# Segment 0's x comes in transposed by three DMA transposes, with wq beside them on ScalarE's queue, in place of four TensorE transposes and one DMA transpose

## The chip, the core and the metric

The kernel runs on one core of a Trainium2 chip. The core has five engines that run side by side, each with its own instruction queue in a fixed order: TensorE (PE, matmuls), VectorE (DVE), ScalarE (ACT, activation functions and copies), GpSimd (POOL) and SyncE (SP, which issues DMAs here). Engines wait for each other by semaphores. The metric is the device time of one execution in microseconds; 262.3 us is the median of three runs before the change, and lower is better.

## The reference

The input x has 2048 tokens of 512 features in bf16. It goes through two branches, and a gate per token mixes their results. Branch a is an attention with a memory, over 4 segments of 512 tokens, with 32 heads of 16 features; branch b is a gated feed-forward layer.

```python
q, k, v = x @ wq, x @ wk, x @ wv            # split into 32 heads and 4 segments of L = 512
for s in range(4):
    logits = einsum('bhqd,bhkd->bhqk', qs, ks) * scale + mask   # mask: only earlier keys
    a_dot = softmax(logits) @ vs
    a_mem = (phi(qs) @ M) / (phi(qs) @ z + 1e-6)
    o = g_head * a_mem + (1 - g_head) * a_dot
    M, z = M + phi(ks).T @ vs, z + phi(ks).sum()
a = concat(o) @ wo
b = (relu(x @ W_gate) * (x @ W_up)) @ W_down
g = sigmoid((x * gate_w).sum(-1))
return g * a + (1 - g) * b
```

## The kernel before

**Layout.** P is 128, D is 512, F is 1792, NC = 4 is the number of 128-row chunks of D. A matmul contracts over the 128 partitions, so the projections need x with features on the partitions: xT[seg % 3] holds one segment as 128 partitions by 4 chunks by 512 tokens. The natural layout, xn (tokens on the partitions), is needed only for the token gate: gate_tasks (L441) multiplies it by gate_w on DVE (L447), four instructions per segment.

**What is computed from xT.** proj_q, proj_k and proj_v (L567, L596, L626) make Q, K and V of a segment, with four accumulating matmuls of 512 columns for each 128 output rows, one per chunk of D. The sum lands in one of the 8 PSUM banks, and a copy on DVE or ACT brings it to SBUF and frees the bank (QT at L588, ktr at L606, Vp at L637). K is then spread into KT by three masked products on DVE (L609). attention (L718) has, for each group u of eight heads, score matmuls (L685, visits of 8 or more small matmuls, on row tiles of PE), exponentials on ACT (L714), a causal mask on POOL (L730) and the product with V on column tiles of PE (L757). ffn_tasks (L915) computes the two hidden projections of branch b from xT, multiplies them on DVE into hT (L931), and out_tile (L942) sums W_down and wo in one bank, scales it (L961) and writes a tile of the output.

**How the order is made.** The kernel does not issue instructions as the Python code runs. Each piece of work is a Task, added to a Plan with its engine and its dependencies. ORDER (L31) is a list of all task numbers, written out by hand, and UNITS (L97) a string that says which buffer or PSUM bank each task's slot takes. Plan.run emits the tasks in that order, which fixes each engine's own order. A matmul task that is marked flexible and stands between column-tiled work is emitted as four column tiles of 32 output rows (L497) and otherwise as one whole matmul (L493). LANDS (L272) holds the times at which the loads were expected when the order was made; it emits nothing.

**The loads.** DMAs at the start are issued in the order of the code, before any task. SP's queue has, in this order: half 0 of xn (tokens 0 to 255, features 0 to 255), wq chunk 0, the first half of wk, wq chunks 2 and 3, a DMA transpose of features 256 to 511 of segment 0 into xT, the second half of wk, wv, the first pieces of W_gate and W_up (g0, u0), gate_w, beta, g1, u1, the rest of xn (all tokens, features 256 to 511), the DMA transpose of segment 1, and the last pieces of W_gate and W_up. ACT's queue has tokens 256 to 511 of xn's first features and wq chunk 1.

**The start of segment 0.** PE first runs seven matmuls on constants (heat, L1002). Then x0_tasks (L522) turns features 0 to 255 on PE: eight matmuls of 128 columns against an identity (L531), each pair into one PSUM bank, a filler matmul of 256 columns on zeros (L540), and four copies, two on DVE and two on ACT (L546), that bring the banks to xT. proj_q for segment 0 runs chunk 0 for all four output groups, then chunk 1, both from the turned half; chunks 2 and 3 wait for the DMA transpose and stand behind K matmuls that use the first two chunks.

## Time and profile before

| | |
|---|---|
| median of 3 runs | 262.3 us (261.94 to 262.34) |
| the profiled execution, its own time | 262.61 us |
| span of that execution in the profile | 260.9 us |
| busy: PE, DVE, ACT, POOL | 97%, 77%, 70%, 26% of the span |
| first matmul, start of the last matmuls | 0.84 us, 257.72 us |
| moved by DMA | 19.75 MB, mean 76 GB/s |

The span goes from the first to the last event that the profiler recorded; the execution's own time has some 1.7 us around it. Busy time is the union of an engine's instructions. Records of consecutive matmuls overlap (at L493 they are mostly 0.38 us long and start 0.215 us apart), so the distance between starts, not the length, is what each one costs. The chain of the work that ended last is followed back from the end, from each instruction to what released it. A wait is put down to the last of the semaphores that it needed. In the rows of stages there stand, after the stretch and its length, the busy time and number of instructions of PE, of its weight loads, DVE, ACT and POOL, then the granted clock, the share of the 16 DMA engines and their GB/s.

### The profile page before, as it was taken

What the parts mean: (1) busy time and instruction counts of PE and PEld (TensorE: products, weight loads), DVE (VectorE), ACT (ScalarE), POOL (GpSimd) and SP (SyncE); (2) the same over time, 40 slices, a digit from 0 to 9 for tenths busy, and PEclk for the clock granted to TensorE, in tenths of its full rate; (3) what the DMA queues carried; (4) which work ended last, traced back from release to release, by engine and by line L of the source; (5) the groups of instructions that cost most, each with busy time, mean ns of one, the idle gap of its engine ahead of it and who ended that gap; (6) DMA issues with size and microseconds to landing.
All of it is one profiled execution on the core that took longest, in us unless ns stands there. A gap on an engine that the chain in (4) does not pass through costs nothing.

```text
span 260.9 us, 9058 instructions
## 1 busy us (share of the span) xinstructions
PE 254.1 (97%) x3914; PEld 120.7 (46%) x3942; DVE 202.1 (77%) x452; ACT 183.0 (70%) x186; POOL 67.3 (26%) x188
## 2 busy tenths in 40 slices
PE   8999999999999999999999999999999999999995
PEld 3444444444545444454545444444545444445445
DVE  2499889999888957998998894697888736596622
ACT  3199899998889678797377837989477875793000
POOL 8018742224322213113021242124112422112000
PEclk9999999999999999999999999999999999999999
DMA  7999963030006243300016541000000043000011
GB/s 194 314 284 259 283 140 105 3 68 13 3 23 132 64 114 75 68 3 3 15 35 107 167 110 57 4 0 8 14 0 10 7 145 112 0 3 3 3 40 43
DMA packets 31600, 19.75 MB, mean 76 GB/s; under 512 B 16072, under 2 KB 30024, under 8 KB 31560
## 3 DMA queue, kind: packets, MB, share of 16 engines
q1 hardware_dynamic: 31144, 18.90, 28.6%
q8 instruction: 31, 0.51, 0.9%
q10 hardware_dynamic: 416, 0.26, 0.3%
q14 instruction: 9, 0.07, 0.1%
HBM read 13.21 MB, written 2.55 MB: 60 GB/s over the span
## 4 chain that ended last, share of the span: by engine, by line
PE 97%; issue 1%; DVE 0%
PE ps L493 53%; PE ps L497 25%; PE ps L685 9%; PE ps L757 7%; PE ps L1006 1%; PE ps L880 1%; PE ps L855 0%; PE ps L531 0%; PE ps L814 0%; DVE osr L961 0%; PE ps L540 0%
## 5 line engine op out<-in xcount | busy, mean ns | idle before, releaser
L714 ACT ACTIVATE E<-ps 128x2048 bf16<-128x2048 f32 (+3 forms) x79 | 120.4, 1552 | 26.4 <-PE ps L685 25.6
L730 POOL TENSOR_SCALAR_AFFINE_SELECT E<-E 128x256 bf16<-128x256 bf16 x128 | 53.7, 448 | 155.0 <-ACT E L714 149.1
L931 DVE TENSOR_TENSOR hT<-ps,rgr 128x512 bf16<-128x512 f32 x56 | 37.8, 681 | 21.9 <-PE ps L493 13.5
L925 ACT ACTIVATE rgr<-ps 128x512 bf16<-128x512 f32 x56 | 32.7, 596 | 20.3 <-PE ps L493 11.1
L493 PE MATMUL ps<-xT,wu_sb 128*128 128x512 bf16 x158 | 41.9, 380 | 0.6 <-issue 0.5
L493 PE MATMUL ps<-xT,wg_sb 128*128 128x512 bf16 x132 | 34.9, 379 | 0.6 <-issue 0.3
L493 PE MATMUL ps<-wd_sb,hT 128*128 128x512 bf16 (+2 forms) x147 | 29.5, 339 | 1.4 <-issue 1.3
L685 PE MATMUL ps<-QT,KT 32*128 32x64 bf16 (+3 forms) x768 | 27.8, 244 | 0.0
L788 DVE STREAM_TRANSPOSE T<-ps 128x512 f32<-128x512 f32 x32 | 21.9, 701 | 3.5 <-PE ps L757 3.1
L497 PE MATMUL ps<-wd_sb,hT 128*32 128x512 bf16 x384 | 24.0, 380 | 0.0
L493 PEld LDWEIGHTS <-wu_sb 128*128 128x128 bf16 x164 | 14.9, 98 | 18.5 <-issue 2.5
L497 PE MATMUL ps<-xT,wg_sb 128*32 128x512 bf16 x344 | 23.1, 380 | 0.0
L685 PEld LDWEIGHTS <-KT 32*128 32x128 bf16 x768 | 11.0, 92 | 24.1 <-issue 22.8
L961 DVE TENSOR_SCALAR osr<-ps,ngcol 128x512 bf16<-128x512 f32 (+2 forms) x18 | 12.2, 682 | 11.3 <-PE ps L493 10.4
L493 PEld LDWEIGHTS <-wg_sb 128*128 128x128 bf16 x138 | 12.9, 98 | 15.7 <-issue 1.3
L493 PEld LDWEIGHTS <-hT 128*128 128x128 bf16 x156 | 13.5, 98 | 14.1 <-issue 2.3
L757 PE MATMUL ps<-E,Vp 128*17 128x320 bf16 (+3 forms) x512 | 19.1, 273 | 0.0
L714 ACT ACTIVATE Em<-ps 128x2048 bf16<-128x2048 f32 (+2 forms) x11 | 15.6, 1415 | 4.3 <-PE ps L685 4.1
L497 PE MATMUL ps<-xT,wu_sb 128*32 128x512 bf16 x240 | 16.2, 379 | 0.0
L588 DVE CAST QT<-ps 128x512 bf16<-128x512 f32 x16 | 10.9, 684 | 6.0 <-PE ps L493 5.5
L493 PE MATMUL ps<-xT,wq_sb 128*128 128x512 bf16 x49 | 14.3, 407 | 0.2 <-issue 0.2
L493 PE MATMUL ps<-wv_sb,xT 128*128 128x512 bf16 x54 | 13.9, 379 | 0.4 <-issue 0.3
(100 smaller groups left out, 308.7 us busy)
## 6 DMA issues: line engine op xcount, KB each, us to landing
out_dram<-osr SPq DMA_DIRECT2D x15, 128.0 KB
xn<-in_A_x_dram SPq DMA_DIRECT2D x3, 512.0 KB
xn<-coefs SPq DMA_DIRECT2D x6, 256.0 KB
cdr<-coefs SPq DMA_DIRECT2D x6, 256.0 KB
wg_sb<-in_B_W_gate_dram SPq DMA_DIRECT2D x2, 512.0 KB
wu_sb<-in_B_W_up_dram SPq DMA_DIRECT2D x2, 512.0 KB
wd_sb<-in_B_W_down_dram SPq DMA_DIRECT2D x2, 512.0 KB
wg_sb<-in_B_W_gate_dram SPq DMA_DIRECT2D x2, 384.0 KB
```

The lines of the kernel that those rows point to most:

```text
L493: nc.tensor.matmul(out, lhsT=lhsT, rhs=rhs, start=start, stop=stop)
L497: nc.tensor.matmul(out[r], lhsT=lhsT[:, r], rhs=rhs, start=start, stop=stop, tile_position=(0, 32 * j))
L588: prj["q", seg, c] = plan.add("DVE", 600, key - RQK, lambda: nc.vector.tensor_copy(QT[i][:], bank(sl)), [a] + war, DVL, frees=[sl])
L685: nc.tensor.matmul(ps[:, o:o + w], lhsT=lhsT.rearrange("p h q -> p (h q)"), rhs=rhs, start=True, stop=True, tile_position=(32 * j, 0))
L714: lambda n0=n0, n1=n1, u=u, f=f, j0=j0, j1=j1: nc.scalar.activation(target(u, f, j0, j1), ps[:, banks[n0] * L:(banks[n0] + n1 - n0) * L], ...
L730: nc.gpsimd.affine_select(out=m[:, :, o:o + HP], in_=m[:, :, o:o + HP], compare_op=ALU.is_ge, fill=0.0, base=HP, pattern=[[0, 4], [1, HP]] ...
L757: nc.tensor.matmul(bank(sl)[32 * m:32 * m + HW, q:q + w], lhsT=(Vp[i] if n < 4 else Vm)[:, kb, r, 4 * c + j, 0:HW], rhs=rhs, start=(n == 0 ...
L788: done.append(plan.add("DVE", 633, key - RL, lambda r=r, sl=sl: nc.vector.transpose(T[ts.i][:, r], bank(sl)), [a] + done, 75 if r else 0, ...
L880: nc.tensor.matmul(bank(sl)[32 * j:32 * j + 32, 34 * g:34 * g + 34], lhsT=pK[i][:, t, g * P + 32 * j:g * P + 32 * j + 32], rhs=Vp[i][:, t, ...
L925: r = plan.add("ACT", 478, key - RL, lambda sl=gsl, rs=rs: nc.scalar.activation(rgr[rs.i][:], bank(sl), ACT.Relu), [g], ACL, frees=[gsl])
L931: nc.vector.tensor_tensor(hT[hs1.i][:], bank(sl), rgr[rs.i][:], ALU.mult)),
L961: nc.vector.tensor_scalar(osr[os.i][:, n0 - c0:n1 - c0], bank(sl)[:, 0:n1 - n0], ngcol[:, tt:tt + 1], None, ALU.mult)),
```

## The change

- x of segment 0 comes to xT by three DMA transposes on SP's queue, of 128, 128 and 256 features (HEAD), ahead of everything else there. The eight transposing matmuls, the filler, the four copies and the identity on POOL are gone, with x0_tasks.
- All of wq is issued by ACT's queue, in three DMAs of one, one and two chunks.
- Behind the transposes SP's queue keeps its order from wk on, and the two halves of wk follow each other. xn is loaded once, whole, in the place where its second half was.
- Q of segment 0 has one task per chunk and output group, each waiting for its chunk of xT and its chunk of wq; in the new order all 16 Q matmuls come first, then K.
- ORDER and UNITS are new throughout: 1354 tasks instead of 1362. LANDS is new for the loads of the start.

```diff
@@ -29,79 +29,79 @@
 ORDER = """
...
 UNITS = (
...
@@ -269,9 +269,9 @@
-    LANDS = dict(n0=3470, n1=3600, q0=4640, q1=4640, ka=6350, q2=7150, q3=7150, x0=8150,
-                 kb=9000, v=10600, g0=12100, u0=13600, gw=14100, be=14400, g1=15600, u1=17100,
-                 n2=18000, x1=21200, g2=22200, u2=23400, g3=24600, u3=25800)
+    LANDS = dict(t0=3700, q0=3700, t1=4300, q1=4300, q2=5400, q3=5400, t2=5600, t3=5600, ka=6600,
+                 kb=7500, v=9200, g0=10900, u0=12600, gw=13100, be=13400, g1=14700, u1=16200,
+                 n0=18000, x1=21200, g2=22200, u2=23400, g3=24600, u3=25800)
@@ -290,6 +290,7 @@
+    HEAD = [(0, 1), (1, 1), (2, 2)]
@@ -306,20 +307,21 @@
-    halves = slice(0, D // 2), slice(D // 2, D)
-    got_n[0] = [load_x0(eng, 2 * t, 2 * t + 2, halves[0], "n%d" % t)
-                for t, eng in enumerate((nc.sync, nc.scalar))]
-
-    def load_wq(eng, ci):
-        return load(eng, wq_sb[:, ci, :], A_wq[ci * P:(ci + 1) * P, :], "q%d" % ci)
-
-    got_q = [load_wq(nc.sync, 0), load_wq(nc.scalar, 1)]
+    def load_wq(ci, n):
+        nc.scalar.dma_start(out=wq_sb[:, ci:ci + n, :], in_=A_wq.rearrange(
+            "(c p) n -> p c n", p=P)[:, ci:ci + n, :])
+        return [arrival("q%d" % (ci + k)) for k in range(n)]
+
+    def load_x0T(ci, n):
+        nc.sync.dma_start_transpose(out=xT[0][:, ci:ci + n, :], in_=x[0:L, ci * P:(ci + n) * P])
+        return [arrival("t%d" % (ci + k)) for k in range(n)]
+
+    got_t, got_q = [], []
+    for ci, n in HEAD:
+        got_t += load_x0T(ci, n)
+        got_q += load_wq(ci, n)
+    got_x[0] = [got_t[0:2], got_t[2:4]]
     got_k = [load_rows(nc.sync, wk_sb, A_wk, 0, "k")]
-    nc.sync.dma_start(out=wq_sb[:, 2:NC, :],
-                      in_=A_wq.rearrange("(c p) n -> p c n", p=P)[:, 2:NC, :])
-    nc.sync.dma_start_transpose(out=xT[0][:, NC // 2:NC, :], in_=x[0:L, halves[1]])
-    got_x0b = arrival("x0")
-    got_q += [arrival("q%d" % ci) for ci in range(2, NC)]
     got_k.append(load_rows(nc.sync, wk_sb, A_wk, 1, "k"))
@@ -328,7 +330,7 @@
-    got_n[0].append(load_x0(nc.sync, 0, NC, halves[1], "n2"))
+    got_n[0] = [load_x0(nc.sync, 0, NC, slice(0, D), "n0")]
@@ -352,10 +354,6 @@
-    ident = sb([P, P], BF16, "ident")
-    nc.gpsimd.memset(ident[:], 0.0)
-    nc.gpsimd.affine_select(out=ident[:], in_=ident[:], compare_op=ALU.not_equal,
-                            fill=1.0, base=0, pattern=[[-1, P]], channel_multiplier=1)
@@ -519,38 +517,6 @@
-    def x0_tasks():
...
@@ -574,13 +540,9 @@
-            for ci in range(2):
-                a = matmuls(K(-8 + ci, c), [got_q[ci]] + x0_first[ci], sl, [
-                    lambda ci=ci: (wq_sb[:, ci, c * P:(c + 1) * P], xT[0][:, ci, :])],
-                    prev=a, start=not ci, stop=False)
-            for ci in range(2, NC):
-                a = matmuls(K(-6 + ci, c), [got_q[ci]] + got_x[0][1], sl,
-                            [proj_mm(wq_sb, c, 0)[ci]], prev=a, start=False, stop=ci == NC - 1)
+            for ci in range(NC):
+                a = matmuls(K(-8 + ci, c), [got_q[ci], got_t[ci]], sl, [proj_mm(wq_sb, c, 0)[ci]],
+                            prev=a, start=not ci, stop=ci == NC - 1)
```

## The prediction

> **What bounds the kernel now.** I read the page first, for the bound, then the waits grouped by who waited for whom.

> ```profile
> span 260.9 us, 9058 instructions
> PE 254.1 (97%) x3914; PEld 120.7 (46%) x3942; DVE 202.1 (77%) x452; ACT 183.0 (70%) x186; POOL 67.3 (26%) x188
> PE 97%; issue 1%; DVE 0%
> PE ps L493 <- issue: 2.5, 16, 0.2
> PE ps L1006 <- PEq L1057: 0.8, 1, 0.8
> ```

> TensorE (PE) is busy for 254.1 of 260.9 us and makes up 97% of the chain that ended last. In the list of waits PE stands still for only two reasons: 0.8 us before its first instruction, and 2.5 us in 16 small gaps of at most 0.2 us. No matmul waits for VectorE (DVE), ScalarE (ACT), GpSimd (POOL) or a transfer. So the end moves only if PE gets less work, does it at another rate, or begins to wait. The change sits in the first microseconds, so I read those instruction by instruction.

> ```profile
> 0.80 0.48 ACTq L280 DMA_DIRECT2D xn<-in_A_x_dram  x1
> 0.80 0.47 SPq L280 DMA_DIRECT2D xn<-in_A_x_dram  x1
> 0.84 2.82 PE L1006 MATMUL ps<-const-bfloat16-1.0 128*128 128x512 bf16 x7 [0.84 <-PEq L1057]
> 3.50 0.77 PEld L531 LDWEIGHTS <-xn 128*128 128x128 bf16 x8 [0.42 <-DMA xn<-in_A_x_dram]
> 3.50 1.04 PE L531 MATMUL ps<-ident,xn 128*128 128x128 bf16 x8
> 3.94 0.85 DVE L546 CAST xT<-ps 128x256 bf16<-128x256 f32 x2 [2.32 <-PE ps L531]
> 4.33 0.42 PE L540 MATMUL ps<-junk 128*128 128x256 bf16 x1
> 4.57 3.00 PE L493 MATMUL ps<-xT,wq_sb 128*128 128x512 bf16 x8
> 5.40 0.15 PEld L493 LDWEIGHTS <-wq_sb 128*128 128x128 bf16 x1 [0.28 <-issue]
> 6.25 0.15 PEld L493 LDWEIGHTS <-wq_sb 128*128 128x128 bf16 x1 [0.28 <-issue]
> 7.41 1.89 PE L493 MATMUL ps<-xT,wk_sb 128*128 128x512 bf16 x8
> 9.13 1.03 PE L493 MATMUL ps<-xT,wq_sb 128*128 128x512 bf16 x4
> 9.84 1.29 DVE L588 CAST QT<-ps 128x512 bf16<-128x512 f32 x2 [5.05 <-PE ps L493]
> 15.27 0.40 PE L685 MATMUL ps<-QT,KT 32*128 32x448 bf16 x8
> ```

> Columns: start, length, engine, line, operation, tiles. The warm-up matmuls on constants (L1006) run until the eight transposing matmuls (L531) can start at 3.50, when the two loads of xn are there (the weight load waits 0.42 for them, under the warm-up); these and the filler (L540) take PE until 4.57, and then the first eight Q matmuls run. PE has two rates here. Weight loads go from 5.40 over one more (5.82) to 6.25, 0.427 us for a matmul of 512 columns; the eight K matmuls take 9.13 - 7.41 = 1.72, or 0.215 each. The eight Q matmuls take 7.41 - 4.57 = 2.84; n at 0.427 and 8 - n at 0.215 give n = 5.3, so PE goes to its full rate at 4.57 + 5.3 x 0.427 = 6.83 us.

> **The change part by part.** *The flips.* Eight matmuls of 128 columns and one of 256 go: 1280 columns, as much as 2.5 Q matmuls (2.5 x 0.427 = 1.07 = 4.57 - 3.50). If PE stays busy and turns at 6.83 as now, a start of Q at T puts (4.57 - T) / 0.427 more matmuls ahead of the turn, and each saves 0.215 afterwards. T = 3.50 gives 0.54 us, T = 4.57 nothing.

> *When x arrives.* The nearest row for a 128 KB DMA transpose on an empty queue is that of pK:

> ```profile
> 132.74 1.21 SPq L622 DMA_TRANSPOSE pK<-pkT  x1
> 133.75:134.00 0.25, 0.25 (x3) 0.10 (x2) 0.25 (x2) 0.25 (x1) 0.18 (x1) 1.00 0.13 22
> 134.00:134.25 0.25, 0.25 (x3) 0.10 (x1) 0.25 (x1) 0.25 (x1) 0.25 (x2) 1.00 1.06 211
> 134.50:134.75 0.25, 0.25 (x3) 0.11 (x2) 0.25 (x2) 0.25 (x1) 0.25 (x2) 1.00 0.39 77
> 2.00:5.40 3.40, 3.40 (x17) 1.63 (x16) 0.85 (x2) 1.90 (x3) 3.20 (x9) 1.00 0.94 302
> ```

> (The last two columns are the share of the 16 DMA engines and GB/s.) Its issue takes 1.21 us, bytes move from 1.1 to 1.9 us after the issue began, at some 213 GB/s. Counted from 0.80, chunk 0's bytes would be in at 2.7. But wq's chunk 0 moves beside it, 256 KB in all as in the two xn loads of before; those, at the 302 GB/s of 2.0 to 5.4, had moved by about 2.9 and released PE at 3.50, 0.6 later. Half of it at 213 instead of 302 GB/s adds at most 128 KB x (1/213 - 1/302), 0.2 us: T between 3.5 and 3.7. I take 3.6: (4.57 - 3.6) / 0.427 x 0.215 = 0.49 us gained. The warm-up ends at about 3.5, so PE stands 0.1 us.

> [...]

> *The next chunks.* SP's queue holds the three transposes one after the other; one of 256 columns has taken 1.33 us to issue:

> ```profile
> 1.83 0.43 SPq L280 DMA_DIRECT2D wk_sb<-in_A_wk_dram  x1
> 2.81 1.33 SPq L320 DMA_TRANSPOSE xT<-in_A_x_dram  x1
> 5.40:6.60 1.20, 1.20 (x4) 0.45 (x3) 0.00 (x0) 0.00 (x0) 1.04 (x8) 1.00 1.25 211
> 7.50:12.20 4.70, 4.70 (x24) 2.09 (x23) 2.36 (x4) 0.00 (x0) 0.00 (x0) 1.00 1.09 347
> 13.25:16.50 3.25, 3.25 (x22) 1.31 (x22) 3.15 (x9) 2.83 (x6) 0.00 (x0) 1.00 1.10 360
> ```

> Issues begin at 0.80, 2.05 and 3.3; by the pK row chunk 1's bytes are in at 4.0 to 4.4, chunks 2 and 3 at some 6.0, and another 0.6 us makes them usable: 5.0 and 6.6. Q needs chunk 1 after four matmuls, at 3.6 + 1.7 = 5.3, and chunk 2 after eight, at 7.0. Both are hidden, by 0.3 and 0.4 us. The dip to 211 GB/s at 5.4 to 6.6, where the one transpose of before ran, says what one costs its neighbours: 0.4 us. Two dips more would make chunk 2 late by 0.4.

> *What is moved behind them.* The first half of wk is issued at 4.7 instead of 1.83, and everything behind it on SP moves too. By bytes, 1.31 MB (x, wq, half of wk) were in at 6.6 before; a second 256 KB transposed adds 0.37: 7.0, usable at 7.6. Q ends at 3.6 + 7.6 x 0.427 + 8.4 x 0.215 = 8.6, so K does not wait. wv is 0.79 MB further at 347 GB/s: 9.3, usable at 9.9; ten K matmuls stand ahead of V now, until 10.8. Behind u1, xn is loaded whole, 256 KB more (0.75 at 347 GB/s), and x of segment 1 and the last weights come 0.75 + 0.37 = 1.1 us later; the instructions ahead of segment 1's first matmul put that at about 25 us, and x of segment 1 is there at about 20. Cost of all this: 0, hidden behind Q and K; without that cover, up to 0.5.

> *Off PE.* Two casts on DVE (0.85), two on ACT, and the identity on POOL go; DVE then waited 5 us for its first QT, so this is worth nothing. ACT issues wq in three DMAs, before it has other work.

> *The new order.* By the two instruction lists PE has 616 whole and 1176 column-split matmuls of 512 columns before (616 + 1176/4 = 910) and 602 and 1232 after (910). Both enter a score visit (L685) 63 times.

> ```profile
> 15.67 2.26 PE ps L493 x10
> 17.93 0.33 PE ps L685 x8
> 12.84 0.54 DVE L609 TENSOR_SCALAR KT<-ktr,mcol_e 128x512 bf16<-128x512 bf16 x2
> 233.81 5.29 PE ps L497 x96
> 257.72 0.39 PE L493 MATMUL ps<-wo_sb,oT 128*128 128x128 bf16 x4
> ```

> Ten whole matmuls take 2.26 us, 24 groups of four split ones 5.29, that is 0.226 and 0.220 each with what a change of mode costs: the exchange is free. The tail after the last matmul at 257.72 has the same tiles. So PE's work differs by the flips alone, and the order can only add waits or take away some of the 2.5 us of gaps. I take 0, with bounds of -0.6 (a quarter of the gaps) and +1.2 (below).

> The first scores come after 16 Q, 10 K, 6 V and 2 K matmuls, at 8.6 + 18 x 0.215 = 12.5 instead of 15.27. Four QT casts, two ktr casts and three KT products precede them on DVE: from about 7.7 at 0.6 per cast, each waiting for its matmuls, and 0.27 per product, KT is ready near 12.4. It fits without reserve.

> *Sum.* The profiled execution took 262.61 us, 1.7 more than its span and 0.3 more than the median of the runs (262.3). 262.61 - 0.49 = 262.12, on the median's scale **261.8 us**.

> **The rivals.** *The order also closes gaps.* The 2.5 us of issue gaps speak for it; that each is at most 0.2 us and belongs to changes of mode, which are as many as before, speaks against. A quarter of them gives 261.8 - 0.6 = 261.2.

> *DVE stands at xn* (slower). The four gate products on xn are in DVE's order, with KT products, hT products that free PSUM banks, and QT casts queued behind them.

> ```profile
> 12.00:14.00 2.00, 1.95 (x10) 0.91 (x10) 2.00 (x7) 1.63 (x3) 0.00 (x0) 1.00 1.00 259
> 16.00:18.00 2.00, 2.00 (x13) 0.80 (x15) 1.90 (x7) 2.00 (x2) 0.00 (x0) 1.00 1.26 207
> 20.38 0.68 DVE L447 SCALAR_TENSOR_TENSOR junk<-xn,gwb 128x512 bf16<-128x512 bf16 x1
> ```

> By bytes, u1 is in at some 16.3 (2.7 MB behind half of wk, at 347 and 360 GB/s, and 0.9 for the dip at 12 to 14, after 7.0) and the whole xn, 0.52 MB, at 17.8, usable at 18.4; the instructions ahead on DVE end at about 18.9 (20.38 before). Reserve 0.5. But the DMA engines have stretches at 259 and 207 GB/s on the way (12 to 14, 16 to 18), and xn must now cross both. If it is usable only at 20.0, DVE, busy nearly all the time here, stands 1.1, PE has no free banks soon after and loses as much: 261.8 + 1.1 = 262.9. It decides against the change where xn comes over 1.0 us later than 18.4, 0.5 for the reserve and 0.5 for the gain. Any other wait that the new order opens on PE has this price too.

> *The full rate comes later.* PE now stands for a moment at 3.5, where it ran on before. If the 6.0 us from its first matmul (0.84) to 6.83 start again at 3.6, the turn comes at 9.6; by then 14 Q matmuls are done, against 5.3 + (9.6 - 6.83) / 0.215 = 18.2 before: 4.2 x 0.215 = 0.9 us lost, 263.2. Against it: the gap is 0.1 us, and the small flips were no denser work. [...]

> *The transposes bring nothing:* x lands at 4.6, as after two dips of 0.4, and PE idles away what it no longer computes: 262.3.

> **How the numbers follow.** Forecast 0.40 (own range 261.4 to 262.1), gaps closed as well 0.17, a wait of DVE or PE 0.24, the rate later 0.13, nothing 0.06. About 0.2%, 0.5 us, is what a measurement of this kernel can tell from no change; the bounds are 261.8 and 262.8. Half of the forecast and the second case are faster: 0.37. Half of the forecast, nothing, and a small wait (0.04) are within: 0.30. The rest is slower: 0.33. The range that leaves out two in ten is 261.1 to 263.3.

> **What would show it.** In the profile of the changed kernel the first Q matmul starts at 3.5 to 3.7, Q ends near 8.6, the first scores stand at about 12.5, and PE's waits still name only issue, with about 2.5 us. Wrong would be: a first Q later than 4.2; matmuls 0.427 us apart beyond 7 us; a wait of PE for a DMA or for DVE; a DVE wait for xn near 18 to 20 us; the last matmul later than 257.7.

## The result and the profile after

| | before | changed |
|---|---|---|
| median | 262.32 us (4 runs, 261.94 to 262.42) | 264.16 us (4 runs, 263.63 to 264.56) |
| ratio of the runs, 95% interval | | 1.0071, 1.005 to 1.0093 |
| the profiled execution, its own time | 262.61 us | 263.63 us |
| its span | 260.9 us | 261.9 us |

The change made the kernel 1.8 us slower; 261.8 was predicted, with a range up to 263.3. The profile is of the fastest of the four runs, 1.0 above the profile of before. From its page and its waits:

```profile
span 261.9 us, 9141 instructions
PE 93%; DMA 2%; SPq 2%; DVE 1%; ACT 1%; issue 0%; ACTq 0%
PE ps L491 <- DMA xT<-in_A_x_dram: 1.5, 2, 0.9
PE ps L491 <- DMA wv_sb<-in_A_wv_dram: 0.6, 1, 0.6
```

Where PE waited for nothing but issue, it now waits for transfers: twice for x and once for wv, 2.1 us in all. Rows of the timeline of the same kernel (start, length, engine, line, operation):

```profile
0.80 1.37 ACTq L311 DMA_DIRECT2D wq_sb<-in_A_wq_dram  x3
0.80 3.89 SPq L316 DMA_TRANSPOSE xT<-in_A_x_dram  x3
0.84 2.83 PE L968 MATMUL ps<-const-bfloat16-1.0 128*128 128x512 bf16 x7 [0.84 <-PEq L1018]
4.56 1.02 PE L491 MATMUL ps<-xT,wq_sb 128*128 128x512 bf16 x4 [0.89 <-DMA xT<-in_A_x_dram]
4.73 1.09 SPq L280 DMA_DIRECT2D wk_sb<-in_A_wk_dram  x2
6.15 2.75 PE L491 MATMUL ps<-xT,wq_sb 128*128 128x512 bf16 x12 [0.57 <-DMA xT<-in_A_x_dram]
8.73 2.32 PE L491 MATMUL ps<-xT,wk_sb 128*128 128x512 bf16 x10
11.68 1.45 PE L491 MATMUL ps<-wv_sb,xT 128*128 128x512 bf16 x6 [0.62 <-DMA wv_sb<-in_A_wv_dram]
13.49 0.40 PE L647 MATMUL ps<-QT,KT 32*128 32x448 bf16 x8
258.73 0.39 PE L491 MATMUL ps<-wo_sb,oT 128*128 128x128 bf16 x4
```

Q starts at 4.56, as late as with the flips (4.57). Chunk 1 is late (6.15) and wv too (11.68). One thing in these rows was not to be expected: the first four Q matmuls fit in 1.02 us, 0.215 apart, so PE was at its full rate by 4.56, where before it turned from half rate (0.427) to full rate at 6.83. The trace's records of the granted clock put this turn at 3.73, and that of the kernel before at 6.84. (In the rows of stages the clock column reads 1.00 before the first such record; the early turn has to be read from the spacing of matmuls.) A second profile of the same kernel, of a run of 264.66 us, is the other way round:

```profile
4.53 6.18 PE L491 MATMUL ps<-xT,wq_sb 128*128 128x512 bf16 x16 [0.86 <-DMA xT<-in_A_x_dram]
4.91 0.15 PEld L491 LDWEIGHTS <-wq_sb 128*128 128x128 bf16 x1 [0.27 <-issue]
9.18 0.15 PEld L491 LDWEIGHTS <-wq_sb 128*128 128x128 bf16 x1 [0.28 <-issue]
9.61 0.61 PEld L491 LDWEIGHTS <-wq_sb 128*128 128x128 bf16 x3 [0.28 <-issue]
10.55 2.32 PE L491 MATMUL ps<-xT,wk_sb 128*128 128x512 bf16 x10
14.53 0.40 PE L647 MATMUL ps<-QT,KT 32*128 32x448 bf16 x8
259.78 0.39 PE L491 MATMUL ps<-wo_sb,oT 128*128 128x128 bf16 x4
```

Here weight loads come one by one, 0.427 us apart, from 4.91 to 9.61; the turn stands at 9.76 in the records. At half rate PE needs chunk 1 only at 6.2 and wv only at 12.7, so those two waits are gone, and it is the rate that costs. The first scores come 1.04 later than in the first profile (14.53 and 13.49), the last matmuls 1.05 later, and the own times differ by 1.03: the whole difference between these two runs of one program was made in their first 14.5 us.

### The profile page after: what moved, and what is told of

The parts are those of the page before. It is cut to its first block, busy times and chain, and to the rows that moved or that the text cites. A ratio compares the mean times of both kernels' runs of the same rounds, so it can differ in the third digit from the quotient of the medians.

```text
span 261.9 us, 9141 instructions
## 1 busy us (share of the span) xinstructions
PE 256.0 (98%) x3975; PEld 119.6 (46%) x3975; DVE 201.1 (77%) x450; ACT 182.9 (70%) x184; POOL 65.8 (25%) x186
## 3 DMA queue, kind: packets, MB, share of 16 engines
HBM read 13.21 MB, written 2.55 MB: 60 GB/s over the span
## 4 chain that ended last, share of the span: by engine, by line
PE 93%; DMA 2%; SPq 2%; DVE 1%; ACT 1%; issue 0%; ACTq 0%
PE ps L491 50%; PE ps L495 26%; PE ps L647 9%; PE ps L719 7%; DMA wv_sb<-in_A_wv_dram 2%; SPq L316 1%; ACT E L676 1%; PE ps L842 1%; PE ps L817 0%; SPq L280 0%; PE ps L776 0%; DVE hT L893 0%; DVE T L750 0%; DVE QT L550 0%; DVE ktr L568 0%
## 5 line engine op out<-in xcount | busy, mean ns | idle before, releaser
L676 ACT ACTIVATE E<-ps 128x2048 bf16<-128x2048 f32 (+3 forms) x79 | 120.7, 1552 | 22.6 <-PE ps L647 20.7
L893 DVE TENSOR_TENSOR hT<-ps,rgr 128x512 bf16<-128x512 f32 x56 | 37.7, 682 | 12.7 <-PE ps L491 8.5
L491 PE MATMUL ps<-xT,wg_sb 128*128 128x512 bf16 x162 | 42.4, 380 | 0.0
L491 PE MATMUL ps<-xT,wu_sb 128*128 128x512 bf16 x152 | 39.9, 380 | 0.1
L495 PE MATMUL ps<-wd_sb,hT 128*32 128x512 bf16 x512 | 31.6, 380 | 0.0
L491 PE MATMUL ps<-wd_sb,hT 128*128 128x512 bf16 (+2 forms) x124 | 23.8, 332 | 0.0
L491 PEld LDWEIGHTS <-wg_sb 128*128 128x128 bf16 x162 | 15.1, 98 | 18.8 <-issue 1.7
L923 DVE TENSOR_SCALAR osr<-ps,ngcol 128x512 bf16<-128x512 f32 (+2 forms) x18 | 12.4, 688 | 14.2 <-PE ps L491 13.1
L495 PE MATMUL ps<-xT,wu_sb 128*32 128x512 bf16 x288 | 20.1, 381 | 0.0
L495 PEld LDWEIGHTS <-hT 128*32 128x32 bf16 x512 | 12.6, 97 | 11.9 <-issue 1.1
L495 PE MATMUL ps<-xT,wg_sb 128*32 128x512 bf16 x248 | 17.3, 380 | 0.0
L550 DVE CAST QT<-ps 128x512 bf16<-128x512 f32 x16 | 10.7, 678 | 7.4 <-PE ps L491 6.8
L491 PE MATMUL ps<-wv_sb,xT 128*128 128x512 bf16 x58 | 15.2, 380 | 0.6 <-DMA wv_sb<-in_A_wv_dram 0.6
L568 DVE CAST ktr<-ps 128x512 bf16<-128x512 f32 x16 | 10.9, 684 | 5.9 <-PE ps L491 3.9
```

Source lines behind the costliest of these rows:

```text
L491: nc.tensor.matmul(out, lhsT=lhsT, rhs=rhs, start=start, stop=stop)
L495: nc.tensor.matmul(out[r], lhsT=lhsT[:, r], rhs=rhs, start=start, stop=stop, tile_position=(0, 32 * j))
L550: prj["q", seg, c] = plan.add("DVE", 600, key - RQK, lambda: nc.vector.tensor_copy(QT[i][:], bank(sl)), [a] + war, DVL, frees=[sl])
L568: d = plan.add("DVE", 600, key - RQK, lambda: nc.vector.tensor_copy(ktr[ks.i][:], bank(sl)), [a], DVL + 40, need=[ks], frees=[sl])
L676: lambda n0=n0, n1=n1, u=u, f=f, j0=j0, j1=j1: nc.scalar.activation(target(u, f, j0, j1), ps[:, banks[n0] * L:(banks[n0] + n1 - n0) * L], ...
L893: nc.vector.tensor_tensor(hT[hs1.i][:], bank(sl), rgr[rs.i][:], ALU.mult)),
```

## The experiments

Theory H puts the loss in the loads of the start, theory O in the new order, theory C in the turn of the clock, theory F in a fixed place of DVE's instructions. Each run stands beside runs of the kernel before on the same chip (medians 262.0 to 262.2).

**New order, old start.** Loads, flips and copies of before in the changed kernel.

```diff
-    for ci, n in HEAD:
-        got_t += load_x0T(ci, n)
-        got_q += load_wq(ci, n)
+    ... xn halves, wq, wk, x0 transpose as before; flips and copies behind heat
```

> The changed kernel's order with the start of the kernel before (xn halves, eight flips, filler and copies on PE, DVE and ACT, wq and wk in the old places of SP's queue). Theory H (the loss sits in the loads of the start: chunk 1 0.73 us late, wv 0.78 us late): both waits go; Q's chunks 2 and 3 come at 7.5 as before, about 0.1 us late for the new order; what is left is the 0.66 us of three waits further back. 262.3 + 0.1 + 0.66 = 263.0, between 262.4 and 263.2. Theory O (the loss sits in the new order): 264.2 as the changed kernel. Theory C (the turn of the clock alone): no difference that holds over the rounds, single runs anywhere from 262.0 to 264.6.

263.25 us, ratio 1.0047 (1.0035 to 1.006), just above the range of theory H. PE has one wait, for the transpose of chunks 2 and 3, which this order needs after eight Q matmuls:

```profile
7.83 1.89 PE L504 MATMUL ps<-xT,wq_sb 128*128 128x512 bf16 x8 [0.63 <-DMA xT<-in_A_x_dram]
```

So the order is not the whole loss, and half of what was lost here (0.63 of 1.27) is a transfer that came 0.3 later than expected.

**The same with that transpose ahead of wk.**

```diff
-    got_k = [load_rows(nc.sync, wk_sb, A_wk, 0, "k")]
     nc.sync.dma_start(out=wq_sb[:, 2:NC, :], ...)
     nc.sync.dma_start_transpose(out=xT[0][:, NC // 2:NC, :], in_=x[0:L, halves[1]])
+    got_k = [load_rows(nc.sync, wk_sb, A_wk, 0, "k")]
```

> The new order with the start of the kernel before, and the DMA transpose of x's second half moved ahead of the first half of wk on SP's queue (issued near 2.3 in place of 2.81). With the transpose behind wk this order lost 1.27, of which 0.63 stood as PE's wait for that transpose at 7.21. Theory H with O small: the wait falls to 0.1 to 0.3 and the time to 262.0 + 0.8 = 262.8, what is left (0.6) being the order's own. Theory H alone: 262.2. Theory O alone: 263.25, unchanged.

262.46 us, 1.0018 (1.0005 to 1.003). PE waits for no transfer:

```profile
4.64 4.60 PE L504 MATMUL ps<-xT,wq_sb 128*128 128x512 bf16 x16
13.06 0.40 PE L660 MATMUL ps<-QT,KT 32*128 32x448 bf16 x8
257.74 0.39 PE L504 MATMUL ps<-wo_sb,oT 128*128 128x128 bf16 x4
```

Its last matmuls start within 0.02 us of those of before (257.72), at nearly the same turn (6.65 in the records, 6.83 before). The order by itself costs between nothing (the two profiles) and 0.4 (the medians). And it is a base to measure against, called the base below: the same order, no wait for a transfer, the old start but for the place of that one transpose.

**Old order, new start.** Transposes and wq as in the change; the old tasks of flips and copies emit nothing.

> The order of the kernel before with the changed kernel's loads (three transposes, wq on ScalarE's queue, no flips). The tasks of the flips and copies emit nothing. Theory H: chunk 1 is 0.7 us late again; after eight Q matmuls stand K matmuls, which need wk at 8.3, so PE waits there for another 0.4 to 1.3 us; 262.3 + 0.7 + 0.4 to 1.3 = 263.4 to 264.3. Theory O: 262.3 as before, or 261.8 with the flips saved. Theory C: no steady difference from before.

264.56 us, 1.0106 (1.0081 to 1.0132), above the range of theory H.

```profile
4.30 1.44 PE L493 MATMUL ps<-xT,wq_sb 128*128 128x512 bf16 x3 [0.63 <-DMA xT<-in_A_x_dram]
6.17 2.29 PE L493 MATMUL ps<-xT,wq_sb 128*128 128x512 bf16 x5 [0.43 <-DMA xT<-in_A_x_dram]
8.25 2.88 PE L493 MATMUL ps<-xT,wk_sb 128*128 128x512 bf16 x8
```

No faster than with the new order (the intervals overlap): the new start loses time whatever follows it. But PE did not stand for wk before K, as was expected; the turn came at 10.26, and PE was too slow to need wk earlier.

**One transpose of 512 columns.** `HEAD` for the transposes is [(0, 4)].

> The changed kernel with one DMA transpose of all 512 columns in place of three. The two alone of 512 KB in the trace of before took 4.0 and 4.2 us from issue to landing. Theory H: all four chunks are usable at 4.9 to 5.4; Q starts 0.3 to 0.8 later than now, chunk 1 costs nothing (0.73 gained), wk and wv are issued some 2 us earlier, so that the wait for wv (0.78) goes: about 264.2 + 0.5 - 0.73 - 0.78 = 263.2. Theory O: 264.2 + 0.5 - 0.73 and no more, 264.0. If instead a transpose is slowed by the wq traffic beside it for as long as it lasts, it lands at 6 or later and the time is 264.5 or above.

265.95 us, 1.014 (1.012 to 1.0161). The time is that of the branch of the slowed transpose, though x was usable at 5.75, between the two branches. PE stood for 2.08 us, and the records put the turn at 8.75, so a late turn is part of this loss too.

```profile
5.75 5.08 PE L493 MATMUL ps<-xT,wq_sb 128*128 128x512 bf16 x16 [2.08 <-DMA xT<-in_A_x_dram]
```

**wq behind the transposes**, on SP's queue, so that nothing moves beside them.

```diff
+    for ci, n in HEAD:
+        nc.sync.dma_start_transpose(out=xT[0][:, ci:ci + n, :], in_=x[0:L, ci * P:(ci + n) * P])
-        nc.scalar.dma_start(out=wq_sb[:, ci:ci + n, :], ...)
+        nc.sync.dma_start(out=wq_sb[:, ci:ci + n, :], ...)
```

> The three transposes alone at the start: wq is issued by SP behind them, so nothing moves beside chunk 0. It is meant for the landing of chunk 0 and loses time in itself, since Q then waits for wq (issued near 4.7, landed near 6.5: about 2 us, so 266 to 267). If wq's traffic makes the first transpose late, chunk 0 lands 2.4 us after its issue, at 3.2, and chunk 1 at 5.0 or earlier; if a transpose at the start of a program is late by itself, chunk 0 lands at 4.5 again and chunk 1 near 6.1.

267.24 us (one run), a little above what was expected. The DMA engines from 0 to 14 us in 40 slices of 0.35 us, in tenths and GB/s:

```profile
DMA  0000006900870189959889999787778999999999
GB/s 0 0 0 0 0 0 159 211 5 10 192 167 5 37 206 233 256 77 240 246 249 334 354 281 325 217 275 269 237 214 228 281 325 334 336 380 345 336 342 363
```

Three bursts with gaps: 2.1 to 2.8, 3.5 to 4.2, 4.9 to 6.1, although the transposes had been issued from 0.80, 2.1 and 3.39. The semaphores of the three are complete at 3.36, 4.75 and 6.71 by the trace, and each burst begins only after the completion before it. Beside wq, in the changed kernel, they are complete at 4.51, 6.11 and 6.84. So with the traffic of the other queue the first came some 1.1 us later (2.56 from issue alone, 3.71 beside wq). It was the completion that was late, not the bytes: by the trace's packets (256 B each for a transpose, 1 KB for a plain load) chunk 0 moved from 2.15 to 2.89 alone and from 2.20 to 3.12 beside wq. Chunk 1 moved from 4.12 on in the changed kernel, as chunk 0 was completing. Chunks 2 and 3 did not wait in this way there: their packets follow those of chunk 1 in one stretch up to 6.32, though chunk 1 is complete only at 6.11.

**A longer warm-up**, over the wait for chunk 0, tests the clock without touching a load.

```diff
-        for k in range(7):
-            w = L if k < 6 else P
+        for k in range(9):
+            w = L if k < 8 else 2 * P
```

It ran beside the changed kernel itself, 264.24 us, 1.0068 (1.0047 to 1.0089), whose profile is the second one above.

> The changed kernel as it is, once more, beside the three others. Theory C (the turn to the full rate comes at the end of a window that runs free of the kernel, a multiple of 3.41 us by the clock's records, if PE was busy in it for some four fifths; the changed kernel stands from 3.67 to 4.56 and mostly spoils that window, so that the turn comes between 7.3 and 10.7 where it came between 3.6 and 7.0 before): the profile before this one, with its turn at 3.73, was a lucky one; most profiles show the turn beyond 7.3 and no wait for chunk 1, and the times scatter over some 1.5 us about 264. Theory H and O: a turn near 3.7 or 6.8 again, waits for chunk 1 (0.7) and wv (0.6 to 0.8) in every profile.

> The changed kernel with the warm-up longer by 1.75 matmuls of 512 columns, to about 4.47, under the wait for chunk 0. Theory C: the turn is back at 3.6 to 7.0; the chunk-1 wait (0.7) and the wv wait show up in every profile, and the time falls by some 0.7, to 263.4, with less scatter. Theories H and O: nothing moves, 264.2, or slower by what the warm-up overruns.

263.67 us, 1.0053 (1.0034 to 1.0072). The medians move as theory C has it, by 0.57, but the intervals overlap. In the profile the turn is at 4.17, and chunk 1 is waited for again. The first scores come at 12.54, 0.52 ahead of the base. By 19 us the lead is gone: ACT stands 0.94 us for beta, a small load further back on SP's queue, and PE then waits for ACT's exponential. So part of what the early turn gained was lost to the next limit (the last two rows).

```profile
0.84 3.63 PE L968 MATMUL ps<-const-bfloat16-1.0 128*128 128x512 bf16 x9 [0.84 <-PEq L1018]
4.36 1.02 PE L491 MATMUL ps<-xT,wq_sb 128*128 128x512 bf16 x4
5.85 2.81 PE L491 MATMUL ps<-xT,wq_sb 128*128 128x512 bf16 x12 [0.47 <-DMA xT<-in_A_x_dram]
15.81 0.23 ACT L423 ACTIVATE eb<-betab 128x32 f32<-128x32 bf16 x1 [0.94 <-DMA betab<-in_A_beta_dram]
18.83 0.40 PE L647 MATMUL ps<-QT,KT 32*128 32x320 bf16 x8 [0.60 <-ACT E L676]
```

**A shorter warm-up in the kernel before**: four matmuls in place of seven, then one.

> The kernel before with four warm-up matmuls in place of seven: PE stands from 2.55 to 3.5, and no load, no order and no later work changes. Theory C: the first window that is busy enough ends between 6.1 and 9.6 in place of 3.6 to 7.0; two to three us more at half rate, half of it lost, 1.2 to 1.3 slower than before: 263.3. Theories H and O: the gap lies before the loads are there and costs nothing, 262.0 to 262.3.

> The kernel before with one warm-up matmul in place of seven: PE stands from about 1.4 to 3.4; loads and order are those of before. The shortening to four matmuls cost nothing; its gap was 0.6 us (2.71 to 3.30), so that a window could still be busy for 83%, as was the one that turned at 3.73 in the changed kernel's first profile, while its second profile with a gap of 0.87 (75%) did not turn. Theory C: with a gap of 2 us no window that ends before 6.2 is busy enough; the turn comes between 6.2 and 9.6, and the time is 1.2 to 1.5 above before, 263.4. If the gap in PE's work has nothing to do with the turn: 262.0 to 262.2, as with four.

With four 261.95 us, 1.0 (0.9974 to 1.0025): expected slower, and it was not. With one 263.27 us, 1.0045 (1.0028 to 1.0061), as expected. One row of each:

```profile
3.30 1.03 PE L531 MATMUL ps<-ident,xn 128*128 128x128 bf16 x8 [0.59 <-DMA xn<-in_A_x_dram]
```

```profile
3.38 1.03 PE L531 MATMUL ps<-ident,xn 128*128 128x128 bf16 x8 [1.95 <-DMA xn<-in_A_x_dram]
```

I had reckoned the gap of the first with 0.95 us; it was 0.59, a sixth of 3.41, the step by which the lengths of the clock records differ: 256.00 us in the kernel before, 259.41 and 252.59 in the two profiles of the changed kernel. How full a stretch of 3.41 us had to be in these runs is bounded by four rows of stages (stretch, length, PE busy and its instructions, PE's weight loads, DVE, ACT, POOL, clock, DMA share, GB/s), each ending or not ending in a turn. The first profile of the changed kernel, turned at its end:

```profile
0.32:3.73 3.41, 2.83 (x7) 1.05 (x8) 0.51 (x7) 1.28 (x1) 2.94 (x9) 1.00 0.55 141
```

The second profile, not turned at the end of the first stretch, but of the next:

```profile
2.93:6.35 3.42, 2.56 (x8) 0.99 (x7) 0.00 (x0) 0.55 (x1) 2.87 (x15) 1.00 1.09 245
6.35:9.76 3.41, 3.41 (x10) 1.18 (x8) 0.69 (x1) 0.00 (x0) 0.00 (x0) 1.00 0.89 272
```

The kernel before, not turned at the end of this stretch, but one stretch later:

```profile
0.01:3.42 3.41, 2.58 (x7) 0.87 (x7) 0.51 (x7) 1.28 (x1) 2.57 (x10) 1.00 0.36 111
```

So 83% (2.83 of 3.41) was enough, 75% (2.56 of 3.42) and 76% (2.58 of 3.41) were not. The other profiles agree: all fifteen that have a clock record turned after a stretch with 83% or more, and none after one with 76% or less. A gap of 0.59 leaves 83% (2.82 of 3.41 from 1.30 to 4.71), so that the four warm-up matmuls could still be enough. Their profile cannot show it: it has no clock record, and its eight Q matmuls (4.37 to 7.53), reckoned as in the prediction, put the turn near 7.3, after a full stretch. With one warm-up matmul PE stood for 1.95 us, and the median was 1.2 us longer though nothing else in the kernel changed. A second look at that one:

> The kernel before with one warm-up matmul, looked at once more. Its first profile took 262.41 us with the turn at 6.56, near the early end of what theory C allows; the median of its runs is 263.27. Theory C: the turn comes at another point between 6.2 and 9.6, and the execution's own time follows it by half the distance: 262.41 + 0.5 x (turn - 6.56), with 0.3 for other scatter. So a turn at 8.3 gives 263.3. If the scatter has another cause, time and turn do not move together.

262.64 us with the turn at 6.95: 262.41 + 0.2 = 262.6 was asked for, a step smaller than the scatter allowed. Both looks fell near the early end of the stretch from 6.2 to 9.6, and these two runs took about what the profiled run of the kernel before took with its turn at 6.83 (262.61). A run at 263.8 was not profiled, so that a late turn makes the 1.2 us is argued, not shown, for this kernel.

**wk and wv on ScalarE's queue behind wq**, with the longer warm-up.

```diff
-    got_k = [load_rows(nc.sync, wk_sb, A_wk, 0, "k")]
+    got_k = [load_rows(nc.scalar, wk_sb, A_wk, 0, "k")]
...
-    ... load_cols(nc.sync, wv_sb, A_wv, 0, D, "v")
+    ... load_cols(nc.scalar, wv_sb, A_wv, 0, D, "v")
```

> The longer warm-up as well as wk and wv on ScalarE's queue behind wq, so that they no longer wait for the transposes to complete. Theory C with H: the wait for wv (0.7) goes as well and the turn is early: 264.2 - 0.7 - 0.7 = 262.8; what is left over before is chunk 1 (0.7) and the order's waits. If the extra traffic beside the transposes delays chunk 1 or chunk 2 by as much as it gains, 263.4 as with the longer warm-up alone. Theory O: 264.2.

266.59 us, 1.0189 (1.0153 to 1.0226): with the extra traffic the transposes came late. (In the changed kernel wk's bytes moved from 6.26 on, with the last transpose packet at 6.32 and the third transpose complete only at 6.84.) The profile is of the slowest of the six runs (269.77).

```profile
7.68 1.02 PE L491 MATMUL ps<-xT,wq_sb 128*128 128x512 bf16 x4 [1.62 <-DMA xT<-in_A_x_dram]
12.43 1.87 PE L491 MATMUL ps<-xT,wq_sb 128*128 128x512 bf16 x4 [3.73 <-DMA xT<-in_A_x_dram]
5.64:9.06 3.42, 1.44 (x6) 0.48 (x5) 0.00 (x0) 0.33 (x1) 0.35 (x3) 1.00 1.17 206
9.06:12.47 3.41, 0.04 (x1) 0.04 (x1) 0.00 (x0) 0.00 (x0) 0.00 (x0) 0.50 1.13 223
12.47:15.87 3.40, 3.40 (x9) 1.20 (x9) 1.38 (x2) 0.00 (x0) 0.00 (x0) 0.50 1.10 333
15.90:20.00 4.10, 4.10 (x23) 1.73 (x25) 3.49 (x8) 1.56 (x3) 0.00 (x0) 1.00 1.12 346
```

Chunk 1 is there at 7.68, chunk 2 at 12.43. The last four rows show the clock column change with such stretches: after one that was 42% busy (1.44 of 3.42) it stood at 0.50, through one that was 1% busy (0.04 of 3.41) and a full one, and after the full one it was back at 1.00. (The stretch after the turn in the changed kernel's first profile, 3.73 to 7.14, was 59% busy, 2.02 of 3.41, and kept the full rate.)

**Two transposes of 256 columns**, with a warm-up of ten matmuls.

> The changed kernel with two transposes of 256 columns in place of three, and a warm-up lengthened to about 4.9. Theory H (transposes of one queue run one after another and the wq traffic beside them delays them): chunks 0 and 1 land together near 5.0, chunks 2 and 3 near 6.9; Q starts 0.4 to 0.5 later than with three, and the chunk-1 wait (0.5 to 0.7) goes: 263.67 - 0.2 = 263.5, between 263.2 and 263.9. If the first lands at 5.7 as the single one of 512 columns did, 264.2 or above.

263.07 us, 1.0039 (1.0026 to 1.0053), better than expected: 256 columns were complete at 4.64, little later than 128 (4.18 to 4.51).

```profile
4.68 1.89 PE L493 MATMUL ps<-xT,wq_sb 128*128 128x512 bf16 x8
6.93 1.89 PE L493 MATMUL ps<-xT,wq_sb 128*128 128x512 bf16 x8 [0.36 <-DMA xT<-in_A_x_dram]
```

**Four more instructions on DVE.** The starts of the 63 score visits were laid against those of the base. The seven profiles of the new start in the new order so far keep their distance from 13 to 29 us (but for the one with the longer warm-up, above), then lose 0.41 between 31 and 34 and gain 0.07 near 58. Five of them lose 0.21 near 170; the ones with wq behind the transposes and with wk and wv on ScalarE's queue do not. The other profile with the old start has none of these steps. At 31 us in the changed kernel's first profile:

```profile
29.83 0.61 PE L495 MATMUL ps<-xT,wu_sb 128*32 128x512 bf16 x8
29.98 0.58 DVE L571 TENSOR_SCALAR KT<-ktr,mcol_o 128x512 bf16<-128x512 bf16 x1
30.98 0.69 DVE L893 TENSOR_TENSOR hT<-ps,rgr 128x512 bf16<-128x512 f32 x1 [0.42 <-PE ps L495]
```

The hT product needs the wu matmuls, which end at 30.44, and rgr from ACT, which was done at 30.25, and DVE is free at 30.56; yet it starts at 30.98. (The releaser in brackets is inferred: PE's wk matmuls happen to end there, and hT does not use them.) The order and the data are those of the base, where no time lies between. One thing that differs is how many instructions DVE has had before.

```diff
     nc.vector.memset(junk[:, 0:P], 0.0)
+    for _ in range(4):
+        nc.vector.memset(junk[:, P:P + 2], 0.0)
```

> The changed kernel with four more tiny memsets on DVE at the start, where DVE waits until 7.6 anyway. In every profile of the new order without the flips DVE begins one hT product 0.42 late near 31 us, although what it waits for was signalled 0.48 earlier, and PE loses 0.41 between 31 and 34 and 0.21 near 170; in the two profiles of the same order with the flips (which have four more DVE instructions) there is neither. Theory F (a stall at a fixed place in DVE's instruction stream, 64 of its instructions from its start): the place moves to an instruction with slack, the steps at 31 to 34 go, and the time falls by 0.3 to 0.4, to 263.8; the step near 170 stays or moves. Rival (the loads of the new start do it, or the order's own waits): both steps stay and the time with them, 264.2.

263.45 us, 1.0051 (1.0037 to 1.0065).

```profile
29.94 0.58 DVE L573 TENSOR_SCALAR KT<-ktr,mcol_o 128x512 bf16<-128x512 bf16 x1
30.53 0.69 DVE L895 TENSOR_TENSOR hT<-ps,rgr 128x512 bf16<-128x512 f32 x1
```

The stall is gone, and with it the step from 31 to 34; the step near 170 stays. It is the trace that shows this, not the time: the median lies 0.8 below that of the changed kernel, twice what the step is worth, the intervals overlap, and the turn came at 5.79 in this profile. The last run puts the memsets beside the two transposes, with the warm-up's columns in 16 matmuls:

> Two transposes and the longer warm-up (263.07, +1.0) with the same four memsets, and the same 4864 warm-up columns in 16 matmuls in place of ten, so that DVE and PE have as many instructions ahead of Q as with the flips. Theory F for both engines: the 0.41 near 31 to 34 and the 0.21 near 170 go, 262.5 (ratio 1.0015 to 1.002). F for DVE alone: 262.7. Rival: 263.07, ratio 1.004.

262.84 us, 1.0037 (1.0022 to 1.0052): by its ratio the rival's case (1.004). In the profile there is again no step at 31, but its first scores come 0.34 later than with the two transposes alone (chunk 2 at 7.27, not 6.93), which cancels the gain. 0.23 is still lost near 170, so PE's count of instructions is not the cause of that step.

The step near 170 has the same look, on ACT. The same exponential in the changed kernel's first profile and in the base:

```profile
168.51 1.88 ACT L676 ACTIVATE E<-ps 128x2048 bf16<-128x2048 f32 x1 [0.54 <-PE ps L647]
```

```profile
167.45 1.88 ACT L689 ACTIVATE E<-ps 128x2048 bf16<-128x2048 f32 x1 [0.26 <-PE ps L660]
```

The trace also records the end of the wait for PE's scores: 0.04 us before the start in the base, 0.32 before it in the changed kernel. Counted over all of the engine's records in the trace, waits and DMA issues included, it is ACT's 192nd instruction in the changed kernel and its 193rd in the base. The late hT product is DVE's 64th, and the 68th with four memsets; 192 is three times 64. In the two profiles without the step, the exponential is the 189th and the 195th. The gain near 58 fits as well: there it is the base whose 64th instruction on ACT starts 0.35 late. So all three steps stand at places in an engine's instruction stream. Most other multiples of 64 show no such delay, ACT's count was not varied by itself, and what the engines wait for stays open.

## Why the prediction was wrong

**The step that failed** is "T between 3.5 and 3.7. I take 3.6" with "PE stands 0.1 us". Chunk 0 was usable at 4.5 (4.56 and 4.53). The working took the transpose's bytes from the pK row and then let it complete 0.6 us after them, as the plain xn loads of before do, with 0.2 more for wq beside it. The bytes were nearly right (the last packet at 3.12); the completion was not. Alone, chunk 0 is complete at 3.4, 0.5 after its last packet; beside wq at 4.51, 1.4 after it. In all six profiles with three transposes beside wq it is complete 0.17 to 0.24 us after wq's second DMA (4.34 here); whether that one holds it up, the traces do not say. So the flips were removed for nothing (Q at 4.57 and 4.56), and PE stood for 0.9 us in the middle of its warm-up.

**The turn**: "If PE stays busy and turns at 6.83 as now" fell with it. The rival that the full rate comes later named what the second profile shows: it set the turn at 9.6, and the profile has 9.76. That the figures are so near is luck. The rival let 6.0 us start again when the gap ends, which from 4.53 would give 10.5, while the stretches in the traces do not start with the kernel or with the gap: the same program turned at 3.73 too. It got 13 in 100 because the gap was taken as 0.1 us. Against the base (Q from 4.64, turn 6.65), the second profile starts Q 0.11 earlier and turns 3.11 later; half of that is lost, 1.56, and 1.56 - 0.11 = 1.45, where its first scores stand 14.53 - 13.06 = 1.47 later. In the kernel before, 1.95 us without PE work cost 1.2 us in the median by itself. That the stretches last 3.41 us and do not start with the kernel is read from these profiles: their clock records (256.00, 259.41 and 252.59 us) are 75, 76 and 74 times 3.413, and the turn came at 3.73 and 9.76 in two runs of one program.

**"Both are hidden"** was wrong too, by the same kind of error. Chunk 1's bytes did not follow its issue at 2.1: they moved from 4.12 on, as chunk 0 completed. It came at 6.15 for 5.3. Chunks 2 and 3 were on time (6.84 for 7.0 at the predicted rate). wv, "usable at 9.9", came at 11.6. In the five profiles with these loads it was complete between 10.68 and 11.63. So some 0.8 us of the lateness is common to all of them; in the first profile the rest is one straggler. Of the 16 steps in which the semaphore of wv counts up, 15 were there by 10.31, before PE needed wv, and the last came at 11.63. With the longer warm-up all 16 were there at 10.68, and PE did not wait. In the first profile these two show: the first four matmuls end at 4.56 + 4 x 0.215 = 5.42, so 0.73 for chunk 1, and the ten K matmuls at 8.73 + 10 x 0.215 = 10.88, so 0.80 for wv. Against the base that is -0.08 for the start, -1.0 for the early turn, +0.73 and +0.80: 0.45, and its first scores are 13.49 - 13.06 = 0.43 late. In the second profile the late turn hides both. In these two the losses are alternatives: the run pays for the transfers or for the clock.

**"K does not wait"** holds, and so does "it fits without reserve" for KT in the order's start. **The new order** at 0 is right to within 0.4. **DVE** did not stand at xn in the changed kernel. The last sentence of that rival priced any other wait that opens on PE. Time was lost on PE, through the late hT product on DVE and the late exponential on ACT, by a cause that was not thought of: 0.41 - 0.07, and 0.21 more near 170, 0.55 in all. For the first profile the sum is 0.43 + 0.55 = 0.98, and its last matmuls stand 258.73 - 257.74 = 0.99 behind the base. For the second it is 1.47 + 0.55 = 2.02; its last matmuls stand 259.78 - 257.74 = 2.04 behind the base and 2.06 behind the kernel before.

**Where the time went, by what was undone:** 1.0068 for the changed kernel, 1.0053 with the gap filled, 1.0039 with two transposes besides, 1.0018 with the old start (each against the kernel before on its own chip). Each step is no larger than its interval; their sum is. No version ran faster than the kernel before. Of the signs named beforehand, four showed: a first Q after 4.2, matmuls 0.427 apart beyond 7 us (in the second profile), PE waiting for a DMA, and the last matmul after 257.7.

## What to carry to other kernels

The start of a kernel is one budget of latency: here a DMA transpose was usable when its completion arrived (4.51), not when its bytes did (3.12). The second transpose on the queue moved only as that completion came in (4.12), and the plain loads behind them when the transposes' bytes were nearly through (6.26). Two transposes of 256 columns (1.0039) were better here than three chunks meant to arrive in turn (1.0053, both with a longer warm-up); one of 512 (1.014) was not. Work on TensorE in the first microseconds may look like waste and yet keep PE busy enough for the full rate (83% of 3.41 us was enough here, 75% was not); whoever removes it must fill the gap, or may pay as here, where the turn came at 9.76 instead of 6.65. Take a second profile of a short start before explaining the first: here two runs of one program lost their time in different places.
